# Attention and gated FFN on one core: both gates of a batch's last two FFN chunks ahead of both values, the gates in the output banks

## The chip, the cores and the metric

One core of one Trainium2 chip. The metric is the device time of one execution in microseconds (us). "PE" is the TensorE matmul row of the trace, "PEld" its weight loads, DVE VectorE, ACT ScalarE, POOL GpSimd.

## The reference, cut to what matters

```python
# q, k, v: 8 batches x 8 heads x 576 tokens x 64; 16 beacon keys and values per head
scores = scale * q @ concat(beacon_k, k)^T      # causal but for the beacons
a = softmax(scores)
x = (a @ concat(beacon_v, v)) -> (8 * 576 tokens, 512)
out = (gelu(x @ w_gate) * (x @ w_val)) @ w_out  # 512 -> 1536 -> 512
```

## The kernel before

Everything is bf16 with fp32 accumulation. For each batch the kernel computes scores, exps, attention and then the gate/value products of one block of 512 tokens (there are nine; the ninth follows the last batch): 12 feature tiles, called chunks 0 to 11 here, each with four gate and four value matmuls of 512 columns. The output matmuls ("o") of the previous block of tokens are spread through the next batch's attention, to keep PE at work while ACT makes the exps.

The matmuls write to PSUM, of which the kernel uses eight banks. Three two-bank buffers, pool "s", hold scores and gate/value pairs; one bank "t" and one bank "o" hold output tiles, transposes and attention results in turn:

```python
psum_s = ctx.enter_context(tc.tile_pool(name="psum_s", bufs=3, space=bass.MemoryType.PSUM))
psum_t = ctx.enter_context(tc.tile_pool(name="psum_t", bufs=1, space=bass.MemoryType.PSUM))
psum_o = ctx.enter_context(tc.tile_pool(name="psum_o", bufs=1, space=bass.MemoryType.PSUM))
```

The last chunk of a batch, chunk 11, is split: its gate goes to "t", its gelu is issued, and only then come the value matmuls. So the gelu, and the table load that exp needs after it, can begin before the values are done.

```python
def gv_mms(ci, fi, *kks, split=False, last=False):
    ...
    part(0)                                    # gate matmuls
    if not split:
        part(1)                                # value matmuls
    ...
    act(ge_sb, gv_of[ci, fi][0], ACT.Gelu)
    if split:
        part(1)
    ...                                        # DVE: hT = value * gelu
```

The start of the next batch, and the end of the loop:

```python
    if b:
        keep(nc.scalar.preload_act_table_set(SET_EXP))
        o(3, b > 1)                            # o matmuls, for b > 1 as 64-row halves
        scores(b, (0, 0))
        scores(b, (0, 2))
        scores(b, (0, 1))
        o(5 if b == 1 else 9, b > 1)
        ...
        ahead(2)                               # batch 1 only: POOL issues two loads of batch 2
        scores(b, (0, 3), (1, 3))
        scores(b, (1, 0))
        scores(b, (1, 2))
        ahead(2)                               # in later batches none is left to issue
        o(5 if b == 1 else 6)
        av_head(b, 0, 0, psum_t, "t")
    ...
    for fi in range(F_TILES):
        if fi >= 2:
            gate_val(b, fi, fi == F_TILES - 1 and b < B - 1)
        if b == 0 and fi in (4, 6, 8):
            transpose_wide(1, (fi - 4) // 2)   # batch 1's q and k, by PE
```

transpose_wide puts K in the "t" bank, emptied by five DVE copies, and Q in the "o" bank, emptied by four ACT copies.

The softmax here doesn't subtract the row's maximum and nothing guards it: scores larger than these inputs give would overflow.

Of the kernel before, what the change touches and what calls it, by code (L numbers as in the profile page):

```python
# [7 lines left out]
P = 128  # L8
B, H, S, NB, D = 8, 8, 576, 16, 64
# [4 lines left out]
F_TILES = D_FF // P  # L14
K_CHUNKS = D_MODEL // P
CH = 512
# [24 lines left out]
FP32 = mybir.dt.float32  # L41
BF16 = mybir.dt.bfloat16
ACT = mybir.ActivationFunctionType
ALU = mybir.AluOpType
# [5 lines left out]
def kernel(  # L50
# [12 lines left out]
    nc = tc.nc  # L63
    keep = tc.keep_in_program_order
# [6 lines left out]
    fpool = ctx.enter_context(tc.tile_pool(name="fpool", bufs=3))  # L71
    hpool = ctx.enter_context(tc.tile_pool(name="hpool", bufs=2))
    opool = ctx.enter_context(tc.tile_pool(name="opool", bufs=2))
# [3 lines that stand above are left out]
# [6 lines left out]
    wg_sb = const.tile([P, K_CHUNKS, D_FF], BF16, name="wg_sb", tag="wg_sb")  # L83
    wv_sb = const.tile([P, K_CHUNKS, D_FF], BF16, name="wv_sb", tag="wv_sb")
    wo_sb = const.tile([P, F_TILES, D_MODEL], BF16, name="wo_sb", tag="wo_sb")
    xT_sb = const.tile([P, NPAIR, N_TOK + P - KROWS[4]], BF16, name="xT_sb", tag="xT_sb")
# [80 lines left out]
    def mm(out_ap, lhsT, rhs, start, stop, **kw):  # L167
        keep(nc.tensor.matmul(out_ap, lhsT, rhs, start=start, stop=stop, **kw))  # L168

    def act(out_ap, in_ap, func, **kw):  # L170
        keep(nc.scalar.activation(out_ap, in_ap, func, **kw))  # L171
# [17 lines left out]
    def transpose_pe(b, m, by_act=False):  # L189
        t_ps = psum_s.tile([P, 2, 1024], BF16, name="t_ps", tag="s")  # L190
        for w in range(2):
            tr_part(b, m, w, t_ps[:, w, :])
        out_ap = qkT[:, m, :, NB:SK].rearrange("p w (t r) -> p w t r", r=6)
        in_ap = t_ps[:, 0:2, 0:S].rearrange("p w (r t) -> p w t r", r=6)
        keep(nc.vector.tensor_copy(out_ap[:, 1], in_ap[:, 1]))
        if by_act:
            act(out_ap[:, 0], in_ap[:, 0], ACT.Copy)
        else:
            keep(nc.vector.tensor_copy(out_ap[:, 0], in_ap[:, 0]))
        keep(nc.vector.tensor_copy(qkT[:, m, 1, 0:NB], t_ps[:, 1, S:SK]))  # L200
# [59 lines left out]
    def scores(b, *parts):  # L260
        s_ps = psum_s.tile([P, 2, 512], FP32, name="s_ps", tag="s")
        c0 = 0
        for m, c in parts:
            score_mms(b, m, c, s_ps[:, :, c0 : c0 + CHUNK_W[c]])
            c0 += CHUNK_W[c]
        (m, c), n = parts[0], len(parts)
        o, w = CHUNK_OFF[c], CHUNK_W[c]
        act(
            exp_ring[:, m : m + n, :, o : o + w].rearrange("p g h c -> p h g c"),
            s_ps[:, :, 0 : n * w].rearrange("p h (g c) -> p h g c", g=n),  # L270
            ACT.Exp,
            scale=QK_SCALE,
        )
        if b:
            for m, c in parts:
                masks(b, m, c)
# [87 lines left out]
    def av(b, m):  # L364
        x = psum_s.tile([P, 2, 512], FP32, name="x_ps", tag="s")
        for hi in range(2):
            attend(b, m, hi, x[:, hi, :])
        normalize(b, m, x, 0, 2)

    def av_head(b, m, hi, pool, tag):  # L370
        x = pool.tile([P, 1, 512], FP32, name="x_ps", tag=tag)
        attend(b, m, hi, x[:, 0, :])
        normalize(b, m, x, hi, hi + 1)
# [10 lines left out]
    def turn_dma(b, m):  # L384
        y_sb, y_before = y_of[b * NPAIR + m], y_of.pop((b - 1) * NPAIR + m)
        keep(nc.vector.tensor_copy(y_sb[0:NB, 0, :, :], y_before[KROWS[4] - NB : KROWS[4], 4, :, :]))
        c0 = b * S - NB
        keep(
            nc.sync.dma_start_transpose(
                out=xT_sb[:, m, c0 : c0 + 5 * P].rearrange("p (j n) -> p j n", n=P),  # L390
                in_=y_sb.rearrange("p j e d -> p (j e d)"),
            )
        )
# [3 lines left out]
    def hold(b, m):  # L397
        x = xT_sb[:, m, b * S : (b + 1) * S]
        keep(nc.gpsimd.tensor_copy(hold_sb, x[:, 0 : S : S - 1]))  # L399
# [9 lines left out]
    h_of, o_of = {}, {}  # L409

    gv_of = {}

    def gv_mms(ci, fi, *kks, split=False, last=False):
        if (ci, fi) not in gv_of:
            if split:
                gv_of[ci, fi] = (
                    psum_t.tile([P, CH], FP32, name="g_ps", tag="t"),
                    psum_s.tile([P, 2, CH], FP32, name="v_ps", tag="s")[:, 0, :],
                )
            else:  # L420
                gv_ps = psum_s.tile([P, 2, CH], FP32, name="gv_ps", tag="s")
                gv_of[ci, fi] = (gv_ps[:, 0, :], gv_ps[:, 1, :])
        n0 = ci * CH

        def part(w):
            for kk in kks:
                mm(
                    gv_of[ci, fi][w],
                    (wg_sb, wv_sb)[w][:, kk, fi * P : (fi + 1) * P],
                    xT_sb[:, kk, n0 : n0 + CH],  # L430
                    kk == 0,
                    last and kk == kks[-1],
                    skip_group_check=True,
                )

        part(0)
        if not split:
            part(1)
        if not last:
            return  # L440
        ge_sb = fpool.tile([P, CH], BF16, name="ge_sb", tag="ge_sb")
        act(ge_sb, gv_of[ci, fi][0], ACT.Gelu)
        if split:
            part(1)
        if ci not in h_of:
            h_of[ci] = hpool.tile([P, F_TILES, CH], BF16, name="hT_sb", tag="hT_sb")
        keep(
            nc.vector.tensor_tensor(  # L448
                out=h_of[ci][:, fi, :], in0=gv_of.pop((ci, fi))[1], in1=ge_sb, op=ALU.mult
            )  # L450
        )

    def gate_val(ci, fi, split=False):
        gv_mms(ci, fi, *range(K_CHUNKS), split=split, last=True)

    def out_mm(ci, ti, fi, o_ps, c0=0, c1=D_MODEL):
        mm(
# [47 lines left out]
    def out_mms(ci, u0, u1):  # L505
        for u in range(u0, u1):
# [19 lines left out]
            out=eye,  # L526
# [25 lines left out]
    def ahead(n):  # L552
        for load in loads[:n]:
            load()
        del loads[:n]
# [52 lines left out]
    for b in range(B):  # L608
        u = [0]

        def o(n, halves=False):
            (out_half_mms if halves else out_mms)(b - 1, u[0], u[0] + n)
            u[0] += n

        if b:
            keep(nc.scalar.preload_act_table_set(SET_EXP))
            o(3, b > 1)
# [4 lines that stand above are left out]
            if b == 1:  # L622
                transpose_pe(1, 3)
                o(5)
            ahead(2)
# [3 lines that stand above are left out]
            ahead(2)  # L629
            o(5 if b == 1 else 6)  # L630
            av_head(b, 0, 0, psum_t, "t")
            o(1)
            scores(b, (1, 1))
            scores(b, (2, 0))
            scores(b, (2, 2))
            ahead(2)
            av_head(b, 0, 1, psum_t, "t")
            turn_dma(b, 0)
            o(7)
            scores(b, (2, 1))  # L640
            scores(b, (2, 3), (3, 3))
            scores(b, (3, 0))
            av_head(b, 1, 0, psum_o, "o")
            o(5)
            av_head(b, 1, 1, psum_o, "o")
            turn_dma(b, 1)
            scores(b, (3, 1))
            scores(b, (3, 2))
            av(b, 2)
            turn_dma(b, 2)  # L650
            o(6)
            av(b, 3)
            turn_dma(b, 3)
            o(11)
            keep(nc.scalar.preload_act_table_set(SET_GELU))
            for kk in range(K_CHUNKS):
                for fi in range(2):
                    gv_mms(b, fi, kk, last=kk == 3)
        for fi in range(F_TILES):
            if fi >= 2:  # L660
                gate_val(b, fi, fi == F_TILES - 1 and b < B - 1)
            if b == 0 and fi in (4, 6, 8):
                transpose_wide(1, (fi - 4) // 2)
            if fi == 0:
                if b and b + 1 < B:
                    hold(b, 3)
                    load_v(b + 1)
                if b and b + 2 < B:
                    load_qk(b + 2)
                if 2 <= b + 1 < B:  # L670
                    transpose_dma(b + 1)
                store(nc.sync)
# [40 lines left out]
```

## Time and profile before

| | before |
|---|---|
| time | 366.15 us median of 3 runs at the time of the prediction |
| span of the profile | 364.1 us |
| PE busy | 353.7 us, 97% |
| PE's wait for an exp | six times, once in each of the batches 2 to 7 |
| period of a later batch | 38.95 us |

The lines are shown in the prediction. In a timeline the columns are start, length, engine, line and operation, output<-input, shapes and count, and in brackets the idle time before it with what ended it. In a view of waits they are the waiter, what it waited for, the total in us, how often, and the longest. PE is so nearly full that only its own gaps count. A matmul's end is estimated, so gaps are counted below from start to start: the time to the next matmul less the 0.216 us that a 512-column one takes in a stream (in proportion for fewer columns: 0.027 us for the 65 of an attend matmul, which multiplies exps with v). The names: qkT transposed q and k, s_ps scores, expT exps, x_ps attention, g_ps, v_ps and gv_ps gates and values, ge_sb gelus, hT_sb value times gelu, o_ps outputs; _ps stands for PSUM. L168, L171 and L111 are the lines of helpers through which all matmuls, ACT operations and loads by POOL go.

### The profile page before, as it was taken

The numbers are of one execution on the slowest core, as the hardware profiler recorded it, in microseconds if no ns is written. First come the engines' busy times: TensorE is split into PE (matmuls) and PEld (weight loads), VectorE is DVE, ScalarE is ACT, GpSimd is POOL, SyncE is SP. The second block draws the span as 40 slices with busy tenths as digits, with TensorE's granted clock in tenths as the row PEclk, the third lists the DMA queues.
The fourth block names the chain that finished last, engine by engine and source line by source line (L and its number), as shares of the span: only waits on it lengthen the run. The fifth ranks groups of instructions, "written<-read, shape, count | busy, mean of one in ns | idle before, by whom it ended". The sixth has DMA issues, their size and how long they took to land.

```text
span 364.1 us, 7726 instructions
## 1 busy us (share of the span) xinstructions
PE 353.7 (97%) x3164; PEld 184.8 (51%) x3206; DVE 162.8 (45%) x320; ACT 192.7 (53%) x252; POOL 161.2 (44%) x288
## 2 busy tenths in 40 slices
PE   7899999999999999999999999999999999999996
PEld 6665446444654455445644464446544564444443
DVE  4547836344443345434534354334444453333332
ACT  3975788237923594349623891379335953321210
POOL 8934497655537552945375455565330530000000
DMA  7999999899179945999299917991797253000102
GB/s 105 173 203 204 198 126 99 129 170 188 23 126 147 215 45 76 163 215 64 56 148 221 111 38 121 170 198 27 112 136 136 17 60 115 0 2 29 58 36 110
DMA packets 160419, 41.57 MB, mean 114 GB/s; under 512 B 146944, under 2 KB 155904, under 8 KB 160384
## 3 DMA queue, kind: packets, MB, share of 16 engines
q0 software_dynamic: 104848, 19.11, 68.9%
q1 hardware_dynamic: 55536, 21.96, 30.7%
q8 instruction: 25, 0.41, 0.5%
q14 instruction: 10, 0.08, 0.1%
HBM read 38.27 MB, written 9.44 MB: 131 GB/s over the span
## 4 chain that ended last, share of the span: by engine, by line
PE 80%; DMA 8%; POOL 6%; ACT 3%; issue 2%; DVE 0%; ACTq 0%; POOLq 0%
PE gv_ps L168 42%; PE o_ps L168 21%; PE x_ps L168 8%; PE s_ps L168 6%; DMA wo_sb<-in_moe_w_out_dram 4%; DMA qk<-in_q_dram 4%; ACT expT L171 3%; POOL qk L111 1%; PE g_ps L168 1%; PE v_ps L168 1%; POOL v_sb L111 1%; POOL q_sb L111 1%; POOL wg_sb L111 1%; POOL wv_sb L111 1%; POOL expT L320 1%
## 5 line engine op out<-in xcount | busy, mean ns | idle before, releaser
L171 ACT ACTIVATE ge_sb<-gv_ps 128x512 bf16<-128x512 f32 x101 | 59.4, 597 | 141.8 <-PE gv_ps L168 139.5
L448 DVE TENSOR_TENSOR hT_sb<-gv_ps,ge_sb 128x512 bf16<-128x512 f32 x101 | 69.0, 691 | 111.6 <-ACT ge_sb L171 109.2
L168 PE MATMUL gv_ps<-xT_sb,wg_sb 128*128 128x512 bf16 x402 | 111.2, 379 | 0.5
L168 PE MATMUL gv_ps<-xT_sb,wv_sb 128*128 128x512 bf16 x388 | 107.9, 379 | 0.4
L171 ACT ACTIVATE expT<-s_ps 128x992 bf16<-128x992 f32 (+3 forms) x112 | 100.2, 979 | 7.0 <-PE s_ps L168 6.4
L168 PE MATMUL o_ps<-wo_sb,hT_sb 128*128 128x512 bf16 (+3 forms) x492 | 101.0, 373 | 1.3
L320 POOL TENSOR_SCALAR_AFFINE_SELECT expT<-expT 128x256 bf16<-128x256 bf16 (+1 forms) x140 | 52.2, 391 | 51.2 <-ACT expT L171 50.0
L168 PEld LDWEIGHTS <-wv_sb 128*128 128x128 bf16 x432 | 42.3, 98 | 50.6
L168 PEld LDWEIGHTS <-wg_sb 128*128 128x128 bf16 x432 | 42.1, 98 | 49.9
L168 PEld LDWEIGHTS <-hT_sb 128*128 128x128 bf16 (+1 forms) x516 | 39.5, 97 | 42.4 <-issue 4.1
L168 PEld LDWEIGHTS <-expT 128*128 128x128 bf16 (+1 forms) x960 | 33.6, 97 | 10.0 <-DVE y_sb L356 3.1
L168 PE MATMUL x_ps<-v_sb,expT 128*128 128x65 bf16 (+1 forms) x960 | 37.4, 193 | 0.2 <-POOL expT L320 0.2
L168 PE MATMUL s_ps<-qkT 64*128 64x80 bf16 (+5 forms) x528 | 33.6, 250 | 3.4 <-DVE qkT L239 1.6
L111 POOL DMA_DIRECT2D v_sb<-in_v_dram x40 | 33.6, 859 | 6.0 <-DMA wg_sb<-in_moe_w_gate_dram 1.8
L111 POOL DMA_DIRECT2D k_sb<-in_k_dram x30 | 25.2, 844 | 15.4 <-DMA q_sb<-in_q_dram 10.8
L356 DVE TENSOR_TENSOR y_sb<-x_ps,r_sb 128x320 bf16<-128x320 f32 (+1 forms) x47 | 28.8, 612 | 1.6
L111 POOL DMA_DIRECT2D q_sb<-in_q_dram x30 | 25.3, 879 | 6.4 <-DMA wo_sb<-in_moe_w_out_dram 3.5
L469 DVE COPY o_sb<-o_ps 128x512 f32<-128x512 f32 (+2 forms) x31 | 20.7, 668 | 15.3 <-PE o_ps L168 14.2
L354 DVE RECIPROCAL r_sb<-x_ps 128x5 f32<-128x5 f32 (+1 forms) x47 | 9.6, 204 | 39.1 <-PE x_ps L168 39.1
L168 PEld LDWEIGHTS <-qkT 64*128 64x128 bf16 x528 | 18.1, 95 | 17.2 <-issue 8.9
L399 POOL COPY hold_sb<-xT_sb 128x2 bf16<-128x2 bf16 x6 | 1.1, 186 | 30.8 <-DMA xT_sb<-y_sb 30.8
L471 DVE COPY o_sb<-o_ps 128x512 f32<-128x512 f32 x6 | 4.1, 691 | 15.4 <-PE o_ps L168 15.4
(58 smaller groups left out, 137.9 us busy)
## 6 DMA issues: line engine op xcount, KB each, us to landing
out_dram<-o_sb SPq DMA_DIRECT2D x35, 256.0 KB, 7.0
v_sb<-in_v_dram POOLq DMA_DIRECT2D x24, 128.0 KB, 9.0
q_sb<-in_q_dram POOLq DMA_DIRECT2D x18, 128.0 KB, 12.2
k_sb<-in_k_dram POOLq DMA_DIRECT2D x18, 128.0 KB, 5.8
wo_sb<-in_moe_w_out_dram POOLq DMA_DIRECT2D x3, 512.0 KB, 14.4
wg_sb<-in_moe_w_gate_dram POOLq DMA_DIRECT2D x2, 512.0 KB, 11.9
wv_sb<-in_moe_w_val_dram POOLq DMA_DIRECT2D x2, 512.0 KB, 13.5
v_sb<-in_v_dram POOLq DMA_DIRECT2D x8, 112.0 KB, 5.4
```

The lines of the kernel that those rows point to most:

```text
L111: keep(nc.gpsimd.dma_start(out=out_ap, in_=in_ap))
L168: keep(nc.tensor.matmul(out_ap, lhsT, rhs, start=start, stop=stop, **kw))
L171: keep(nc.scalar.activation(out_ap, in_ap, func, **kw))
L320: nc.gpsimd.affine_select(out=d, in_=d, pattern=[[0, 2], [1, n]], compare_op=ALU.is_ge, fill=0.0, base=0, channel_multiplier=-1,)
L354: keep(nc.vector.reciprocal(r, x[:, :, :, D:DV]))
L356: nc.vector.tensor_tensor(out=y_of[i][:, :, h0:h1, :].rearrange("p j b d -> p b j d"), in0=x[:, :, :, 0:D], in1=r.to_broadcast([P, h1 - h0 ...
L399: keep(nc.gpsimd.tensor_copy(hold_sb, x[:, 0 : S : S - 1]))
L448: nc.vector.tensor_tensor(out=h_of[ci][:, fi, :], in0=gv_of.pop((ci, fi))[1], in1=ge_sb, op=ALU.mult)
L469: keep(nc.vector.tensor_copy(o_ap, o_ps))
L471: keep(nc.vector.tensor_copy(o_ap, o_half))
```

## The change

The intent: with both gates ahead of both values, the last gelu ends earlier, so that the exp table is loaded earlier and the burst of exps of the next batch can start earlier. The o matmuls around the scores stay where they were. The core of the diff:

```diff
+    def gates_first(ci, *fis):
+        ge_of = {}
+        for fi, (pool, tag) in zip(fis, ((psum_t, "t"), (psum_o, "o"))):
+            g_ps = pool.tile([P, CH], FP32, name="g_ps", tag=tag)
+            part(ci, fi, 0, g_ps)
+            ge_of[fi] = gelu(g_ps)
+        for fi in fis:
+            v_ps = psum_s.tile([P, 2, CH], FP32, name="v_ps", tag="s")[:, 0, :]
+            part(ci, fi, 1, v_ps)
+            gated(ci, fi, v_ps, ge_of[fi])
 ...
         for fi in range(F_TILES):
-            if fi >= 2:
-                gate_val(b, fi, fi == F_TILES - 1 and b < B - 1)
+            if fi >= 2 and (fi < F_TILES - 2 or b == B - 1):
+                gate_val(b, fi)
+            if fi == F_TILES - 2 and b < B - 1:
+                gates_first(b, fi, fi + 1)
```

(Cut: gv_mms is taken apart into part, gelu and gated, which changes nothing.)

## The prediction

> **What bounds the kernel now.** I read the page first: busy shares, then the chain that ended last.
>
> ```profile
> span 364.1 us, 7726 instructions
> ## 1 busy us (share of the span) xinstructions
> PE 353.7 (97%) x3164; PEld 184.8 (51%) x3206; DVE 162.8 (45%) x320; ACT 192.7 (53%) x252; POOL 161.2 (44%) x288
> ...
> PE 80%; DMA 8%; POOL 6%; ACT 3%; issue 2%; DVE 0%; ACTq 0%; POOLq 0%
> ```
>
> PE is busy all but 10.4 us, and most of that idle time lies in the first 25 us. From about 53 us on, the chain is PE work almost throughout. So a change gains only where PE waits or runs slowly, and whatever makes PE wait is paid in full. The view of waits, PE only, says where it waits:
>
> ```profile
> PE s_ps L168 <- DVE qkT L239: 1.6, 3, 0.7
> PE w_ps L168 <- DVE idle L80: 1.1, 1, 1.1
> PE s_ps L168 <- ACT expT L171: 0.9, 6, 0.2
> PE s_ps L168 <- ACT qkT L171: 0.7, 1, 0.7
> PE t_ps L176 <- DMA qk<-in_q_dram: 0.3, 1, 0.3
> PE x_ps L168 <- POOL expT L320: 0.2, 1, 0.2
> ```
>
> After the start there are two: a score matmul waits for an exp at six of the seven batch boundaries, and an attend matmul waits once for a mask. The intent of the change must be aimed at the first, so I read the timeline of one such boundary (third to fourth batch, counted from 0):
>
> ```profile
> 162.15 0.60 ACT L171 ACTIVATE ge_sb<-gv_ps 128x512 bf16<-128x512 f32 x1 [1.13 <-PE gv_ps L168]
> ...
> 163.02 0.60 ACT L171 ACTIVATE ge_sb<-g_ps 128x512 bf16<-128x512 f32 x1 [0.27 <-PE g_ps L168]
> 163.63 1.28 ACT L616 ACT_TABLE_LOAD   x1
> ...
> 163.78 0.82 PE L168 MATMUL o_ps<-wo_sb,hT_sb 64*128 64x512 bf16 x6
> ...
> 164.43 0.80 PE L168 MATMUL s_ps<-qkT 64*128 64x512 bf16 x14
> 164.92 1.02 ACT L171 ACTIVATE expT<-s_ps 128x1024 bf16<-128x1024 f32 x1
> ```
>
> The last gelu, the table load and the exps follow one another on ACT without a break; three score blocks fill the three score buffers, and a later score matmul (167.72) waits for the third exp. On the face of it an earlier last gelu should shorten that wait. But the first scores are issued only at 164.43, after six o matmuls: the exp has two predecessors that end at nearly the same time.
>
> The last view is the same place in the first batch, which has three PE transposes in its gate/value stretch:
>
> ```profile
> 40.37 0.43 PE L176 MATMUL t_ps<-eye,qk 96*128 96x96 bf16 x6
> ...
> 41.34 1.95 DVE L218 COPY qkT<-t_ps 64x288 bf16<-64x288 bf16 x4
> ...
> 42.36 1.03 PE L168 MATMUL gv_ps<-xT_sb,wg_sb 128*128 128x512 bf16 x4
> ...
> 43.30 0.17 DVE L222 COPY qkT<-t_ps 128x16 bf16<-128x16 bf16 x1
> ...
> 44.09 1.03 PE L168 MATMUL g_ps<-xT_sb,wg_sb 128*128 128x512 bf16 x4
> ```
>
> Here the K half of the transposes sits in the single "t" bank until the fifth DVE copy ends at 43.47; the gate of chunk 11 takes that bank at 44.09, with 0.6 us to spare.
>
> **What the Trainium skill says.** "ScalarE: Activation LUTs", What ACT_TABLE_LOAD costs, gives about 1283 ns for the load plus about 1380 ns of DRAIN. The trace agrees on the load (1.283 us) and not on the drain: the load begins 17 ns after the gelu ends, and the exp 11 ns after the load. So 1.28 us is all there is to hide. "PSUM — Partial Sum Buffer", Engine vs sequencer instructions: matmuls start in program order, and the ACT and DVE queues are strict FIFO. The trace agrees (starts in program order, never a later matmul past a waiting one); so one gate that waits for its bank holds back all PE work after it. "TensorE: Matmul & The Clock Gate", What's actually happening: it takes an idle window of about 3.4 us to halve the clock. The granted clock is 1.00 in each of the five batches I asked for; a bubble near 1 us should leave it there. "Perfetto Trace Analysis", Tensor Engine Instruction: the profiler estimates a matmul's end. The trace bears it out: a 512-column matmul is shown as 379 ns while its successor starts 216 ns later. So I count PE's losses from start to start: the score wait, shown as 0.15 us, is 167.724 - 167.189 - 0.216 = 0.319 us.
>
> **The change part by part.** Nothing is added or removed: the order view shows 6414 PE rows, 157 ACT rows and 228 DVE rows before and after. At seven boundaries (after the batches 0 to 6) the four matmuls of value 10 and the four of gate 11 change places: gate 10, gate 11, value 10, value 11 instead of gate 10, value 10, gate 11, value 11. Gate 10 goes to the "t" bank, gate 11 to the "o" bank, each value to half a score buffer.
>
> (a) ACT at the six later boundaries. Gate 11 ends four matmuls earlier, 4 x 0.216 = 0.863 us. Its gelu starts at 162.15 instead of 163.02, and the table load ends at 164.05 instead of 164.913. When can the first exp start then? Its scores are issued where they were: second 512-column matmul at 164.436, shown for 376 ns, and ACT's wait record for it is at 164.852. Where ACT has nothing else to do, an exp starts 62 ns after such a record (170.539, exp at 170.601). That gives 164.914, against 164.924 today: 0.01 us gained out of 0.86. The three exps then run back to back as before, and the wait of 0.319 us becomes 0.309. Six times: -0.06 us. The first boundary has no exp wait of this kind, so nothing there.
>
> (b) PE's own joints. The change from value 11 to the half-row o matmuls shows 163.775 - 163.463 - 0.216 = 0.096 us of loss. That looks like the wait for gelu 11 to free the "t" bank (it ended at 163.613), but the same 0.096 us stands at every change between 128-row and 64-row matmuls where nothing is waited for (o to scores at 170.108, s to x at 170.846). I take it to stay: 0.
>
> (c) Buffers in the later boundaries. Values 10 and 11 take the buffers that chunks 10 and 11 took; value 11's product ends at 164.640 as before, and value 10's would run at 163.09 to 163.78, before the score block that takes its buffer (164.65). The "o" bank is empty since the previous batch's last o tile. The three gelu buffers suffice. 0.
>
> (d) The first boundary. Gate 10 now asks for the "t" bank at 42.36, but that bank holds the transposes until the copy of 43.303 + 0.166 = 43.469. The DVE queue cannot be quicker: product 8 and the five copies run without a gap from 40.73. With some 0.05 us for the signal (the masked exp that ended at 52.821 released PE at 52.873), gate 10 starts at about 43.53 rather than 42.36: +1.17 us of idle PE, and program order lets nothing past it. The "o" bank is free by then (ACT's four copies end at 42.82), so gate 11 doesn't wait again.
>
> (e) What of that is given back. In the second batch an attend matmul waits for POOL: issued from 52.873 where the rate would have had it at 52.54, so 0.34 us. POOL is held there by its DMA issues; the masks of the third exp would come about 0.6 us later than now, the two key loads after them too, and the mask awaited would end near 53.43. PE, 1.17 us later, comes at 53.71 and finds it done. The 0.34 us vanishes: -0.34. I find no other PE wait after that which has slack to give.
>
> Sum: -0.06 + 1.17 - 0.34 = +0.77 us, so 366.15 + 0.77 = 366.9 us.
>
> **The rivals.** First, the intended one: the burst moves forward by the whole 0.86 us and the wait of 0.319 us goes at all six boundaries, -1.9 us, with the bubble of (d) in place 365.1, without it 364.2. For it: the ACT run without a break from gelu to the third exp, and the chain, which goes through "ACT expT" there. Against it: the wait record at 164.852, i.e. the scores come no earlier. Second, no bubble: the "t" bank would be free earlier than I think, or the wait is on another copy; then about 366.1. Against it: the order view lists a DVE wait on the first weight load of gate 10 in the changed kernel, and all five copies read that bank. Third, the bubble is paid in full and more: the later exps push POOL's masks and key loads so that an attend matmul waits again, 1.2 to 1.6 us in all, 367.4 to 367.8. For it: POOL is the tightest engine from 46 to 54 us; against it: PE moves by more than POOL does. A product of value 10 that holds up a score block is a lesser one; it has 0.87 us of slack.
>
> **Range and chances.** The three runs of before span 0.5 us, so the number itself is uncertain by some 0.3. I put most weight on (d), a little on the smaller relief of the first rival. Low 366.2, high 367.6. Two per cent is 7.3 us; no path I found moves a third of that. Faster 0.01, same 0.98, slower 0.01.
>
> **What would show it.** Right: span near 364.9; in the waits a new row "PE g_ps", released by the DVE copy of the transposes, once, about 1.0 us (shown from the estimated end of the matmul before); the mask wait of 0.2 gone; the exp wait still six times and about 0.9 in all; ACT's wait for scores grown from 6.4 by six times 0.86 to about 11.5, the table load having moved into idle time. Wrong: the six exp waits gone or halved (then the record at 164.852 isn't the scores' arrival), no gap before gate 10 near 42.4, or a new wait in each later batch, which would show as a period over 38.95 us from one table load to the next.

## The result, and the profile after

The changed kernel took 366.80 us (median of 6 runs, 366.63 to 367.20) against 365.99 us for before (6 runs, 365.57 to 366.58, among them the three known when the prediction was made). The ratio is 1.0023, with a 95% interval of 1.0010 to 1.0036: 0.2% slower, which is "same" at the 2% mark.

The page of the changed kernel, the lines that answer to those of before:

```profile
span 365.1 us, 7733 instructions
...
PE 354.1 (97%) x3164; PEld 185.2 (51%) x3206; DVE 163.0 (45%) x320; ACT 192.6 (53%) x252; POOL 161.2 (44%) x288
...
PE 92%; ACT 3%; DVE 2%; issue 2%; ACTq 0%
```

The span is 1.0 us longer and PE is no busier in any way that matters. The chain that ended last no longer passes through POOL and DMA before 53 us: it now runs along PE and DVE there. That is the first hint that PE became the later one in that stretch. The view of waits, PE only:

```profile
PE s_ps L168 <- DVE qkT L239: 1.6, 3, 0.7
PE w_ps L168 <- DVE idle L80: 1.1, 1, 1.1
PE g_ps L168 <- DVE qkT L222: 1.0, 1, 1.0
PE s_ps L168 <- ACT qkT L171: 0.7, 1, 0.7
PE s_ps L168 <- issue: 0.3, 1, 0.3
```

The row that matters is new: a gate matmul that waits for the transposes' last DVE copy. (The "issue" row lies at 19.4 us, before anything that the change moves.) The row for the exp is gone, but not the wait: from start to start it is still there at all six boundaries, 0.309 to 0.310 us against 0.319 to 0.320. Counted from the estimated end of the matmul before, as the view counts, it was 0.155 us and is 0.145 us now, and the view lists nothing under 0.15 us. The timeline of the first batch shows the new row in place:

```profile
41.50 1.03 PE L168 MATMUL gv_ps<-xT_sb,wv_sb 128*128 128x512 bf16 x4
...
43.30 0.17 DVE L222 COPY qkT<-t_ps 128x16 bf16<-128x16 bf16 x1
...
43.52 1.90 PE L168 MATMUL g_ps<-xT_sb,wg_sb 128*128 128x512 bf16 x8 [1.00 <-DVE qkT L222]
```

PE ends value 9 and stands until the fifth copy has emptied the "t" bank. From start to start it loses 1.160 us. The boundary between batches 3 and 4, which the prediction showed for before, now reads:

```profile
163.17 0.60 ACT L171 ACTIVATE ge_sb<-g_ps 128x512 bf16<-128x512 f32 x1 [0.27 <-PE g_ps L168]
163.78 1.28 ACT L618 ACT_TABLE_LOAD   x1
...
164.79 0.82 PE L168 MATMUL o_ps<-wo_sb,hT_sb 64*128 64x512 bf16 x6
...
165.45 0.80 PE L168 MATMUL s_ps<-qkT 64*128 64x512 bf16 x14
165.93 4.42 ACT L171 ACTIVATE expT<-s_ps 128x1024 bf16<-128x1024 f32 x5 [0.86 <-PE s_ps L168]
```

Against PE, the load is 0.86 us earlier, and ACT then stands for 0.86 us until the scores arrive. In the whole trace ACT's wait for scores has grown from 6.4 to 12.2 us. At this boundary the change made idle time on ACT, and 0.01 us on PE.

The third place is the second batch, where POOL makes the masks and issues the loads. POOL before:

```profile
52.39 1.49 POOL L320 TENSOR_SCALAR_AFFINE_SELECT expT<-expT 128x256 bf16<-128x256 bf16 x4
53.83 1.79 POOL L111 DMA_DIRECT2D k_sb<-in_k_dram  x2
...
58.60 1.76 POOL L320 TENSOR_SCALAR_AFFINE_SELECT expT<-expT 128x256 bf16<-128x256 bf16 x5
```

and after:

```profile
54.65 0.41 POOL L320 TENSOR_SCALAR_AFFINE_SELECT expT<-expT 128x256 bf16<-128x256 bf16 x1 [0.43 <-ACT expT L171]
55.00 1.77 POOL L111 DMA_DIRECT2D k_sb<-in_k_dram  x2
...
59.74 1.42 POOL L320 TENSOR_SCALAR_AFFINE_SELECT expT<-expT 128x256 bf16<-128x256 bf16 x4
```

The loads and the masks after them come 1.17 and 1.14 us later, because a mask ahead of them (at 54.65 here, at 53.48 before) waits for an exp whose scores PE issued 1.17 us late. PE itself had in the meantime won back the mask wait of 0.34 us near 52.9 and was late by 0.82 us only. So it ran into a later mask. The weight loads of the changed kernel show it:

```profile
60.85 0.69 PEld L168 LDWEIGHTS <-expT 128*128 128x128 bf16 x21 [0.16 <-POOL expT L320]
```

From start to start this new wait is 0.203 us. I cut each trace in three by PE's own instructions: from the 16-column transpose of the third transpose_wide (near 40.26) to the first gate matmul of batch 1, from there to the first gate matmul of batch 7, and the rest.

| kernel | third transpose to batch 1's gates | batch 1's gates to batch 7's | to the end |
|---|---|---|---|
| before | 24.80 | 233.70 | 65.39 |
| changed | 25.83 | 233.66 | 65.39 |

The first stretch carries the loss: 1.160 - 0.340 + 0.203 = 1.023, and it is 1.03 us longer. The second has six of the exp waits, 0.01 us shorter each.

### The profile page after: what moved, and what is told of

The parts are those of the page before. It is cut to its first block, busy times and chain, and to the rows that moved or that the text cites. A ratio compares the mean times of both kernels' runs of the same rounds, so it can differ in the third digit from the quotient of the medians.

```text
span 365.1 us, 7733 instructions
## 1 busy us (share of the span) xinstructions
PE 354.1 (97%) x3164; PEld 185.2 (51%) x3206; DVE 163.0 (45%) x320; ACT 192.6 (53%) x252; POOL 161.2 (44%) x288
## 4 chain that ended last, share of the span: by engine, by line
PE 92%; ACT 3%; DVE 2%; issue 2%; ACTq 0%
PE gv_ps L168 44%; PE o_ps L168 22%; PE x_ps L168 9%; PE s_ps L168 7%; PE g_ps L168 3%; PE v_ps L168 3%; ACT expT L171 3%; PE t_ps L176 1%; DVE qkT L235 1%; PE w_ps L168 1%; DVE qkT L218 0%; PE y_ps L176 0%; DVE hT_sb L433 0%; ACT qkT L171 0%; ACT ge_sb L171 0%
## 5 line engine op out<-in xcount | busy, mean ns | idle before, releaser
L171 ACT ACTIVATE ge_sb<-gv_ps 128x512 bf16<-128x512 f32 x94 | 55.2, 597 | 134.4 <-PE gv_ps L168 132.1
L433 DVE TENSOR_TENSOR hT_sb<-gv_ps,ge_sb 128x512 bf16<-128x512 f32 x94 | 64.2, 691 | 104.6 <-ACT ge_sb L171 104.6
L171 ACT ACTIVATE expT<-s_ps 128x992 bf16<-128x992 f32 (+3 forms) x112 | 100.2, 979 | 12.8 <-PE s_ps L168 12.2
L168 PE MATMUL gv_ps<-xT_sb,wg_sb 128*128 128x512 bf16 x374 | 104.1, 379 | 0.5
L168 PE MATMUL gv_ps<-xT_sb,wv_sb 128*128 128x512 bf16 x360 | 100.7, 379 | 0.4
L433 DVE TENSOR_TENSOR hT_sb<-v_ps,ge_sb 128x512 bf16<-128x512 f32 x14 | 9.7, 692 | 11.5 <-PE v_ps L168 11.5
```

The source lines that it names most:

```text
L168: keep(nc.tensor.matmul(out_ap, lhsT, rhs, start=start, stop=stop, **kw))
L171: keep(nc.scalar.activation(out_ap, in_ap, func, **kw))
L433: keep(nc.vector.tensor_tensor(out=h_of[ci][:, fi, :], in0=v_ps, in1=ge_sb, op=ALU.mult))
```

## The experiments

My theory after the result: the bank wait in batch 0, less what the mask waits of batch 1 give back, is the whole loss; the later boundaries gain next to nothing since the first exp waits for its scores, which the change leaves where they were. The rivals: the burst did gain and the bubble hides it; the new order costs something at every boundary; the give-back is not POOL's doing. Nine kernels were run, all correct, on three chips; each ratio is to before in the same rounds. The times are in one table at the end of this section.

### late_only: the six later boundaries alone

```diff
-            if fi == F_TILES - 2 and b < B - 1:
+            elif fi == F_TILES - 2 and b > 0:
                 gates_first(b, fi, fi + 1)
+            elif fi == F_TILES - 2:
+                gate_val(b, fi)
+                gates_first(b, fi + 1)
```

> The changed order at the six later boundaries only; the first boundary (after batch 0) is as in the kernel before. My theory (the later boundaries gain 0.01 us each because the first exp waits for its scores; the bubble before gate 10 in batch 0 and what follows it in batch 1 are the whole loss): no PE wait for the DVE copy, the mask wait of 0.2 us back as before, six exp waits of 0.309 us from start to start, span 0.06 us under before, i.e. same time within 0.1 us. Rival 1 (the exp burst did move and the bubble hides it): 1.0 to 1.9 us faster. Rival 2 (the new order costs something at each boundary): 0.5 us or more slower.

Measured: ratio 0.9995 (0.9972 to 1.0017), span 364.0 us. Its view of PE's waits has no row for the DVE copy; the mask wait is back; ACT stands 0.86 us after each of the six later table loads, and PE's exp wait is 0.308 us at all six:

```profile
PE x_ps L168 <- POOL expT L320: 0.3, 1, 0.3
```

So the later boundaries are worth nothing that can be timed. The interval alone would still allow some 1.0 us of gain or 0.6 us of loss; what rules out rival 1 is the exp wait, and rival 2 the length of the batches: from one batch's gates to the next, 38.94 us for the first five against 38.95 in before. (The sixth takes 39.00 us, with one wait of 0.14 us for DVE's y_sb that the changed kernel does not have in the same place; I have no cause for it.)

### first_only: the first boundary alone

The same edit with `b == 0` in place of `b > 0`.

> The changed order at the first boundary only. My theory: all of the loss: one PE wait for the DVE copy (1.16 us from start to start), the mask wait of 0.34 us given back, a new mask wait of 0.20 us near 60.8; span 1.02 us over before, time about 367.0 where before reads 366.0; six exp waits of 0.319 us as before. Rival 2 (a cost at each later boundary): under 0.5 us slower.

Measured: ratio 1.0027 (1.0002 to 1.0052), span 365.2 us. The exp waits are 0.319 to 0.320 us, as in before. The first stretch is 25.83 us, that of the changed kernel to the hundredth, with nearly the same waits, 1.157 us before gate 10 and 0.198 us near 60.8:

```profile
PE g_ps L168 <- DVE qkT L222: 1.0, 1, 1.0
PE s_ps L168 <- ACT expT L171: 0.9, 6, 0.2
```

The loss is all here.

### swap_banks: gate 10 in the "o" bank, gate 11 in the "t" bank

```diff
-        for fi, (pool, tag) in zip(fis, ((psum_t, "t"), (psum_o, "o"))):
+        for fi, (pool, tag) in zip(fis, ((psum_o, "o"), (psum_t, "t"))):
```

> The changed kernel with the two banks exchanged: gate 10 in the o bank, gate 11 in the t bank, at all seven boundaries. My theory: in batch 0 the o bank holds the Q half of the transposes until ACT's fourth copy, which ended at 42.82, where the five DVE copies of the K half ended at 43.47; so the bubble before gate 10 shrinks from 1.16 to about 0.5 us from start to start, is released by ACT in place of DVE, and gate 11 does not wait. The six exp waits stay 0.309. With the mask wait of batch 1 giving back up to 0.34, the time is 0.1 to 0.4 us over before. Rival (the bubble is not the bank but something else of the new order in batch 0): 1.16 us as in the changed kernel.

Measured: ratio 1.0019 (1.0005 to 1.0032), span 364.5 us.

```profile
42.89 1.89 PE L168 MATMUL g_ps<-xT_sb,wg_sb 128*128 128x512 bf16 x8 [0.34 <-ACT qkT L171]
```

The bubble is 0.508 us from start to start, and ACT's copy of Q ends it. Which bank, and who empties it, sets the size: the cause is shown. The first stretch is 25.16 us, 0.36 over before, and the waits give 0.508 - 0.340 + 0.202 = 0.370.

### before_scores_early and late_scores_early: the scores moved too

For the batches 2 to 7, in the kernel before and in late_only:

```diff
-            o(3, b > 1)
+            if b == 1:
+                o(3)
             scores(b, (0, 0))
             scores(b, (0, 2))
+            if b > 1:
+                o(3, True)
             scores(b, (0, 1))
```

> The kernel before, with the first two score blocks of the later batches issued ahead of the three first o fractions instead of after them (about 0.65 us earlier on PE). My theory: the table load, which still ends where it did, then is the later of the exp's two predecessors: first exp at most 0.01 us earlier, exp waits stay near 0.31, time within 0.15 us of before. Rival (the scores alone set the exp's start): waits gone, 1.9 us faster.

Measured: ratio 0.9996 (0.9973 to 1.0019). The first exp still starts 0.011 us after the table load in each batch, and the exp wait is 0.319 to 0.320 us. Earlier scores alone are worth nothing, just as an earlier table alone is. This run told one thing more, taken up under "what sets the give-back" below.

> late_only with the first two score blocks issued ahead of the three o fractions in the later batches. My theory: both predecessors now are early: table load ends 0.86 us and scores end 0.65 us earlier, the first exp starts about 0.65 us earlier against PE, the six waits of 0.319 us go (needed: 0.32 earlier), 1.9 us faster, about 364.1 where before reads 366.0. Rival (the three exps or a buffer release hold the burst anyway): a wait of another name takes the place of the exp wait, such as a score block waiting for value 10's product, and the gain is under 1 us.

Measured: ratio 0.9983 (0.9961 to 1.0006), not clear of 1. My number, 1.9 us, was wrong. The first half of the reasoning held: the first exp starts 0.22 us after the table load, ended by its scores, and the exp wait is gone from all six batches. But the period shrank only from 38.95 to 38.86 us (38.93 in the last batch, where the wait for y_sb stands again), the second stretch from 233.70 to 233.25 us. The view of PE's waits, and the timeline of one boundary, say where the rest went:

```profile
PE o_ps L168 <- DVE o_sb L473: 1.1, 6, 0.2
```

```profile
166.92 0.69 DVE L473 COPY o_sb<-o_ps 128x512 f32<-128x512 f32 x1 [2.57 <-PE o_ps L168]
...
167.66 1.46 PE L168 MATMUL o_ps<-wo_sb,hT_sb 128*128 128x512 bf16 x5 [0.19 <-DVE o_sb L473]
```

The next output tile wants the "o" bank, and DVE is still copying the half tile out of it. The gap before it is 0.352 us, of which 0.095 stands at every such change from 64-row to 128-row matmuls; 0.257 us of wait has taken the place of 0.319. In the kernel before, this copy ended at 167.90 and the o matmul came at 168.03: the second limit stood just behind the first, and I had not looked for it.

### half_by_act: late_scores_early with that copy on ACT

```diff
-            keep(nc.vector.tensor_copy(o_ap, o_half))
+            act(o_ap, o_half, ACT.Copy)
```

> late_scores_early with the copy that empties the o bank of the half tile (DVE, 0.69 us, begun at 166.92 and awaited by PE until 167.61) given to ACT, which stands idle from 166.72 to 167.16 there and takes about 0.6 us for 512 columns. My theory (PE now waits for that bank alone): the wait of 0.25 us per later batch shrinks by about 0.1 us, period 38.77 instead of 38.87; over six batches 0.6 us, so about 1.0 us faster than before in all. Rival (the copy pushes the fourth and later exps so that PE waits for an exp, a score buffer or a mask again): period 38.87 or longer.

Measured: ratio 0.9975 (0.9961 to 0.9988), 364.85 us against 365.99: this kernel beats before, and with it the changed kernel, though it was not run in the same rounds as that one. At the 2% mark it too is "same". The gap is 0.255 us in place of 0.352, i.e. a wait of 0.16 in place of 0.257, and the second stretch is 232.58 us, 1.1 us under before:

```profile
166.42 0.60 ACT L171 ACTIVATE o_sb<-o_ps 128x512 f32<-128x512 f32 x1 [0.20 <-PE o_ps L168]
...
167.07 1.45 PE L168 MATMUL o_ps<-wo_sb,hT_sb 128*128 128x512 bf16 x6
```

In late_scores_early ACT stood idle from 166.72 to 167.16, and the copy fills that gap. What is left of the wait is ACT's own copy, which ends at 167.02.

### before_loads_later, after_loads_later, combined: the loads issued in batch 1 moved

For batch 1 alone, in the kernel before, the changed kernel and late_scores_early:

```diff
-            ahead(2)
+            ahead(2 if b > 1 else 0)
             scores(b, (0, 3), (1, 3))
             scores(b, (1, 0))
             scores(b, (1, 2))
-            ahead(2)
+            ahead(2 if b > 1 else 4)
```

> The kernel before; in batch 1 alone, the two key loads that POOL issues ahead of the mask of the fourth exp are issued four instructions later, together with the next two. My theory of the give-back (the attend matmul near 52.9 waits for a mask that POOL makes after those loads): that wait of 0.34 us goes, 0 to 0.35 us faster, unless the four loads in one go hold up a later mask, which would show as a PE wait for POOL near 58 to 61. Rival (the wait hangs on ACT or PE): it stays.

Measured: ratio 1.0056 (1.0033 to 1.0079), slower. The wait near 52.9 is gone: the mask that it was for now ends at 52.14 and waits for its exp in place of the loads. This run alone does not show that the edit did it, for POOL's load of q ahead of those masks started at 46.04 us here and at 46.35 in before; 0.31 us is nearly the whole wait (see "what sets the give-back"). And the four loads in one go hold up later masks, the reservation in the expectation, and cost more than they save: PE loses 0.707 us near 57.5 and then 0.27 and 0.50.

```profile
54.36 2.62 POOL L111 DMA_DIRECT2D k_sb<-in_k_dram  x3
56.96 1.43 POOL L320 TENSOR_SCALAR_AFFINE_SELECT expT<-expT 128x256 bf16<-128x256 bf16 x4
```

> The changed kernel with the same later key loads. My theory: nothing is left to give back, so against before_loads_later in the same rounds it is slower by the whole bubble less the burst's gain, 1.16 - 0.06 = 1.10 us, more than the 0.8 to 1.0 between the changed kernel and before. Rival (the give-back has another source): the difference stays 0.8 or so.

Measured: 368.16 us against 367.28 for before_loads_later, medians of four runs each with ranges of 1.1 and 2.1 us; the timed difference of 0.9 does not tell 0.8 from 1.1. The traces do: both have the same three mask waits (0.705, 0.276 and 0.498 here), and the first stretch is 27.20 against 26.03 us. The difference, 1.17 us, is the whole bubble of 1.161: with nothing to give back, nothing is given back.

> late_scores_early with the later key loads of batch 1. Expected as the sum of the parts: per later batch 0.09 us (period 38.86 instead of 38.95, the exp wait replaced by a wait of 0.25 us for the DVE copy of the half tile), 0.5 us in six, and 0 to 0.35 us from the mask wait: 0.5 to 0.9 us faster than before, some 365.2 where before reads 365.9.

Measured: ratio 1.0021 (1.0008 to 1.0035), slower than before by 0.8 us where 0.5 to 0.9 us of gain were expected. Its second stretch is 233.23 us, the gain of late_scores_early; its first is 26.03 us, the loss of before_loads_later. The sum of the parts holds with the measured size of the load part, whose sign I had wrong.

### What sets the give-back

before_scores_early has the same program as before up to batch 2, yet its first stretch is 24.66 us, not 24.80. Its start took 0.51 us longer (the third transpose at 40.77 instead of 40.26); it has no wait near 52.9 and a wait of 0.202 us near 60.2: -0.340 + 0.202 = -0.138. So the mask waits depend on how late PE comes against POOL in that run. The other traces bear this out. Take the time from the third transpose to POOL's load of q that waited for a DMA (46.35 in before). It is 6.09 us in before and 6.15 in late_only, which have the wait near 52.9, 0.34 and 0.42 us, and first stretches of 24.80 and 24.88 us. It is 5.31 in before_scores_early, 5.71 in late_scores_early and 5.69 in half_by_act, whose program is the same up to the end of this stretch, as late_only's is: all three have no such wait, one of 0.20 near 60, and a first stretch of 24.66 us. The changed kernel takes 25.83 us at 6.10, and first_only the same at 5.25. So against a before whose POOL comes early the change costs 25.83 - 24.66 = 1.17 us, the whole bubble, and swap_banks likewise 25.16 - 24.66 = 0.50; the 1.03 and 0.36 above hold against the one profile of before. In the eleven profiles the third transpose stands anywhere from 39.72 to 40.77 us.

| kernel | median us (range, runs) | ratio to before of the same rounds |
|---|---|---|
| before, first | 365.65 (364.99 to 368.34, 11) | |
| late_only | 365.93 (365.31 to 366.33, 6) | 0.9995 |
| first_only | 366.96 (366.61 to 367.57, 6) | 1.0027 |
| before_scores_early | 365.81 (365.34 to 366.47, 6) | 0.9996 |
| late_scores_early | 365.47 (364.77 to 365.96, 6) | 0.9983 |
| before, second | 365.55 (364.94 to 366.10, 9) | |
| swap_banks | 366.27 (365.99 to 366.53, 4) | 1.0019 |
| before_loads_later | 367.28 (366.91 to 368.97, 4) | 1.0056 |
| after_loads_later | 368.16 (367.77 to 368.85, 4) | 1.0077 |
| combined | 366.46 (365.74 to 366.68, 5) | 1.0021 |
| before, third | 365.99 (365.53 to 366.81, 9) | |
| half_by_act | 364.85 (364.35 to 365.59, 5) | 0.9975 |

## Why the prediction was right

The number, 366.9 us, lies 0.1 from the median measured, 366.80. The steps one by one:

- **(a) The burst** held. Predicted 0.309 us for the exp wait, measured 0.309 to 0.310; the first exp starts on the scores' arrival and ACT stands 0.86 us. late_only shows the sum: no gain that can be timed. (ACT's wait for scores grew to 12.2 us, not 11.5: the first boundary, left out of that figure, adds 0.80.) That it takes both, an earlier table and earlier scores, is shown by before_scores_early and late_scores_early.
- **(b) PE's joint** held. From value 11 to the o matmuls the changed kernel still loses 164.789 - 164.477 - 0.216 = 0.096 us, though gelu 11 is long done.
- **(c) Buffers** held: no later boundary has a new PE wait, and value 11's product causes none.
- **(d) The bubble** held: 1.160 us against 1.17, released by the copy that was named, and swap_banks moved it to the other bank's copies as it should. The granted clock stayed at 1.00 from 42.2 to 46.0 us, as the prediction expected.
- **(e) What is given back** was half right. The 0.34 us near 52.9 did vanish. The step that failed is "PE moves by more than POOL does", said against the third rival. It held at the awaited mask, which came 0.57 us later (0.6 predicted). But three masks on, POOL took over the full 1.17 us, since its masks wait for exps whose scores PE had issued late, while PE kept 0.82. So an attend matmul ran into a later mask for 0.203 us, a wait of the kind that the third rival named, though not of its size. The term is 0.137 us, not 0.34, and the difference of the spans is 1.0, not 0.77. Even so it hangs on the one trace that was read: against three of the four others with the same program there, nothing is given back ("what sets the give-back").

That the number came so close is in part luck. The medians differ by 0.81 us, and the interval of the ratio, 0.4 to 1.3 us, holds 0.77, 1.03 and 1.17 alike: only the traces show that (e) was off. The kernel before also read 0.16 us lower in these rounds than at the time of the prediction. The prediction's counts of rows (6414, 157 and 228) stand in no kept view; the pages give the same counts for both kernels, PE 3164, PEld 3206, ACT 252 and DVE 320, so its point, that nothing is added, holds.

The first rival's size, 1.9 us for a burst that moves, was out of reach of this change, and not of this change alone. late_scores_early made the burst move, and the wait for the "o" bank behind it let 0.45 us through.

What stays open: why the start takes 39.7 to 40.8 us to the third transpose. No run here was made to tell; the time from there to POOL's load, 5.2 to 6.2 us, is open too.

## What to carry to other kernels

An instruction with two predecessors that end within 0.01 us of each other gains nothing from either alone: move both, and look beforehand for the third that stands behind them. A bank that is free at the moment of today's use need not be free one matmul group earlier; follow its last reader in the timeline, above all in the one iteration that differs from the others. A wait that a delay "gives back" may return further on, if the engine that caused it is delayed as well.

## What the Trainium skill lacked or had wrong

- "ScalarE: Activation LUTs", What ACT_TABLE_LOAD costs: of the 1380 ns of DRAIN that it adds to the 1283 ns load, nothing shows in this kernel. The exp started 0.011 us after the load, before the change and also in before_scores_early, where its scores had long been there; the load itself began 0.017 us after the gelu's end.
- "TensorEngine Tiling (Array Packing)", Key Properties, says that a change of the tiling mode drains TensorE, without a figure. Here each change between 128-row and 64-row matmuls at which PE waits for nothing else cost 0.094 to 0.097 us from start to start, in either direction.
- "TensorE: Matmul & The Clock Gate", Back-to-back issue gap, gives some 131 ns per matmul for a sustained stream of weight loads and 512-column matmuls, and 216 ns for an isolated gap. In this kernel the sustained stream runs at 216 ns per matmul.
- No page that I read gives the delay that step (a) rests on: where ACT waits for scores in a separate record, the exp starts 0.062 us after that record. The first exps of the changed kernel, 0.011 us earlier against PE at each boundary, agree with it.
